# Attention operands of a backward pass packed in four groups of 32 rows, with the steps of the inner loop ordered by hand

## The chip, the cores and the metric

The kernel runs on one core of one Trainium2 chip. Times are device microseconds (us) of that core. A time that is quoted is the median of several executions, and "ratio" is always the mean time of one kernel's fast runs over the mean time of the other's fast runs of the same rounds, so it is not quite the ratio of the two medians.

The names of the engines in the profile are: PE is the matmul engine (PEld its weight loads), DVE is VectorE, ACT is ScalarE, POOL is GpSimd, and SP is SyncE.

## The reference

The reference is one transformer-like block and its gradients: `out = x + attention(xn) * silu(mlp(xn))` with `xn = layernorm(x)`, and the vector-Jacobian product of it for one `grad_out`. There are 2048 tokens, 512 features and 32 heads of 16 features. The part that matters here is the attention and its backward pass:

```python
def _A_ref(x, wqkv, wo):
    B, S, D = x.shape          # 1, 2048, 512
    H = 32
    Dh = D // H                # 16
    qkv = (x @ wqkv).reshape(B, S, 3, H, Dh).transpose(2, 0, 3, 1, 4)
    q, k, v = qkv[0], qkv[1], qkv[2]
    scores = jnp.einsum("bhqd,bhkd->bhqk", q, k) * (Dh ** -0.5)
    p = _softmax(scores, axis=-1)
    o = jnp.einsum("bhqk,bhkd->bhqd", p, v)
    return o.transpose(0, 2, 1, 3).reshape(B, S, D) @ wo
# ... layernorm, MLP, silu, and then
_out, _vjp = jax.vjp(_f, A_x, A_wqkv, A_wo, B_w1, B_b1, B_w2, B_b2)
_grads = _vjp(grad_out)
```

## The kernel before

The kernel has three phases: a first one up to about 285 us, the attention core up to about 2400 us, and a last one with the output projection and the weight gradients. The change touches only the attention core.

The core works through 64 blocks (16 pairs of heads times 4 chunks of 512 queries), and a block has 16 steps. Every step does the following, for both heads of the pair:

- `s`: the scores with keys on the rows, two matmuls into a tile of 128x1024 f32 (two PSUM banks). ScalarE makes `et = exp(s)`.
- `t`: the scores of the block before, with queries on the rows. ScalarE makes `e = exp(t)`.
- `d`: dP, the product of V and the output gradient, also 128x1024. VectorE makes `gts = d * et`.
- `X`: six accumulating matmuls, four on `et` and two on `gts`, into one bank for the whole block. At the block's end `X` is copied (`xs`), transposed on PE (`XT`), copied again (`xt`), and weights `W1`, `W2` for the next stage are made of it.
- `Z`: two matmuls on `e` and two on `gk`, which is `gts` transposed by a DMA. Every fourth step VectorE adds `Z` to `acc`.

So a step needs two exponentials of 128x1024, and one multiply of the same size. "The edge" below means positions 0 to 4 of a block, where `X` changes hands. PSUM is the memory that PE writes its results to; the kernel lays it out in 8 banks. A slot is one buffer in it: the next tile of that slot waits until the last one has been read (below, most `d` start 0.05 us after the multiply that reads the one before). A mode is how many rows and columns of PE's array a matmul takes, as the profile prints it: 64\*128 or 32\*128 for `s`, `t` and `d`, 128\*32 or 128\*17 for `X` and `Z`. A change of mode is one between these two kinds.

```python
# PSUM: 8 banks = s 2, (t and d share a ring of two slots) 4, X 1, Z 1
ps_s = ctx.enter_context(tc.tile_pool(name="ps_s", bufs=1, space=PSUM))
ps_x = ctx.enter_context(tc.tile_pool(name="ps_x", bufs=1, space=PSUM))
ps_z = ctx.enter_context(tc.tile_pool(name="ps_z", bufs=1, space=PSUM))
ps_d = ctx.enter_context(tc.tile_pool(name="ps_dt", bufs=2, space=PSUM))
ps_t = ps_d
# ... operands: per head 64 rows, K and V side by side; Q alone, dO alone
KVT=opnd.tile([128, S], bf16, name=f"KVT{i}"),
QT=opnd.tile([128, S], bf16, name=f"QT{i}"),
DOT=opnd.tile([128, S], bf16, name=f"DOT{i}"),

def emit_r1(g):                       # s, t, d of step g
    # ...
        s = ps_s.tile([128, 2, 512], f32, name="s")
        for hj in range(2):
            r0 = 64 * hj
            nc.tensor.matmul(s[:, hj, :], lhsT=op["KVT"][r0:r0 + 64, kb * 128:(kb + 1) * 128],
                             rhs=op["QT"][r0:r0 + 64, qc * 512:(qc + 1) * 512],
                             start=True, stop=True, tile_position=(r0, 0))
    # ...
        t = ps_t.tile([128, 2, 512], f32, name="t", tag="d")       # then two matmuls on QT, KVT
    # ...
        d = ps_d.tile([128, 2, 512], f32, name="d", tag="d")       # then two matmuls on KVT, DOT

def emit_mult(g):
    # ...
    nc.vector.tensor_tensor(out=gts[:, kb % 2], in0=st_d.pop(g)[:], in1=st_et[g], op=ALU.mult)

def emit_finalize(j):                 # at a block's end
    # ...
    XT = ps_x.tile([128, 4, 128], f32, name="XT", tag="X")         # in the one bank of X
    # ... four transposes, copy to xt, then W1 and W2

emit_r1(0)
for g in range(NSTEP + 16 + lagb + laga):
    # ...
    emit_r1(g + 1)                    # s, t, d of the next step
    emit_exp_a(g)                     # et
    emit_mult(g)                      # gts
    emit_exp_b(g)                     # e
    emit_dmat(g)                      # gk by DMA
    # ... X(et) of step g-1, Z, X(gts) of step g-1
```

Around this a scheduler decides the final order on each engine; in this kernel it leaves PE's order as s, t, d, X, Z.

## Time and profile before

| | before |
|---|---|
| time, median of 3 runs | 3007.36 us (3003.35 to 3009.01) |
| first and last start of an `e` exponential | 311.3 and 2391.9 us |
| one block, average | 32.54 us |
| ACT busy from 320 to 2350 us | 1875 of 2030 us |
| one exponential; pitch of two that queue | 1026 ns; 0.90 to 0.92 us |

The first fence shows lines of the page of the profiled execution of the kernel before: busy time and share of each engine, then the row of ACT in tenths in 40 slices, then the three costliest groups. In a group the columns are line, engine, operation, tiles and shapes, count, then busy us and mean ns of one, then idle time of the engine just before and what ended most of it.

```profile
...
PE 2491.3 (83%) x19909; PEld 859.6 (29%) x19968; DVE 2011.0 (67%) x2422; ACT 2205.8 (74%) x2485; POOL 583.2 (19%) x944
...
ACT  2442899998899999999999989999999824441020
...
L701 DVE TENSOR_TENSOR gts<-d,et 128x1024 bf16<-128x1024 f32 x1024 | 1251.5, 1222 | 555.9 <-ACT et L690 534.5
L690 ACT ACTIVATE et<-s 128x1024 bf16<-128x1024 f32 x1024 | 1050.5, 1026 | 161.5 <-PE s L647 126.7
L727 ACT ACTIVATE e<-t 128x1024 bf16<-128x1024 f32 x1024 | 1049.5, 1026 | 6.2 <-PE t L659 5.0
...
```

Over the whole span no engine stands out (PE 83%, ACT 74%). The row by slices says why this average is of no use: from the fifth slice to the 32nd, which is about the attention, ACT is at 80% or more. The windows view of the kernel before gives the same stretch in us; its columns are the window, its length, busy us and count for PE, PEld, DVE, ACT and POOL, then the granted PE clock, the share of the DMA engines and GB/s.

```profile
...
320.00:2350.00 2030.00, 1828.77 (x16108) 540.00 (x16109) 1495.49 (x1608) 1874.98 (x1983) 219.21 (x594) 1.00 0.81 146
...
```

ACT is busy 92% of that window, PE 90%. The exponentials overlap each other by some 0.1 us, so ACT is close to full; the leak is the rest. The waits view of the kernel before for the same window says what the leak is; the columns are total us, number of times, longest.

```profile
...
DVE gts L701 <- ACT et L690: 521.0, 696, 3.3
...
PE t L659 <- ACT e L727: 119.6, 450, 0.5
ACT et L690 <- PE s L647: 117.7, 172, 2.6
...
```

VectorE waits on ScalarE, which is as it should be with ScalarE the limit. The line that counts is the last: ScalarE, the limit, waited 118 us for `s`.

The timeline of the kernel before shows one pair of steps; columns are start us, duration us, engine, line, operation.

```profile
...
1118.60 1.22 DVE L701 TENSOR_TENSOR gts<-d,et 128x1024 bf16<-128x1024 f32 x1
...
1119.17 0.39 PE L647 MATMUL s<-QT_2217,KVT_2216 64*128 64x512 bf16 x2
...
1119.53 0.39 PE L659 MATMUL t<-KVT_2216,QT_2217 64*128 64x512 bf16 x2
...
1119.60 1.02 ACT L690 ACTIVATE et<-s 128x1024 bf16<-128x1024 f32 x1
1119.87 0.39 PE L670 MATMUL d<-DOT_2218,KVT_2216 64*128 64x512 bf16 x2
...
1120.52 1.02 ACT L727 ACTIVATE e<-t 128x1024 bf16<-128x1024 f32 x1
...
1120.66 1.22 DVE L701 TENSOR_TENSOR gts<-d,et 128x1024 bf16<-128x1024 f32 x1 [0.84 <-ACT et L690]
...
1120.96 0.39 PE L647 MATMUL s<-QT_2217,KVT_2216 64*128 64x512 bf16 x2
...
1121.43 1.03 ACT L690 ACTIVATE et<-s 128x1024 bf16<-128x1024 f32 x1
1121.59 0.39 PE L659 MATMUL t<-KVT_2216,QT_2217 64*128 64x512 bf16 x2 [0.24 <-ACT e L727]
...
1121.93 0.39 PE L670 MATMUL d<-DOT_2218,KVT_2216 64*128 64x512 bf16 x2
...
1123.02 0.39 PE L647 MATMUL s<-QT_2217,KVT_2216 64*128 64x512 bf16 x2
...
```

The first `s` at 1119.17 is followed by `t` 0.36 us and `d` 0.70 us later, and the next `s` is 1.79 us after it; but the third `s`, at 1123.02, comes 2.06 us after the second. And `t` at 1121.59 starts 0.05 us after the exponential of 1120.52 ends. Between 700 and 2000 us, 87% of all `d` start 0.053 us after the end of a multiply, and 87% of all `t` start 0.052 us after the end of an `e`.

### The profile page before, as it was taken

How to read it: one execution, taken by the hardware profiler on the slowest of the kernel's cores; microseconds unless marked ns; L12 is line 12 of the kernel's file. 1: busy time of each engine (PE TensorE's matmuls, PEld its weight loads, DVE VectorE, ACT ScalarE, POOL GpSimd, SP SyncE). 2: the span in 40 equal slices, each digit the busy share in tenths (PEclk: the TensorE clock that was granted, in tenths of full speed). 3: DMA queues.
4: the chain of work that ended last, by engine and by line, in shares of the span. 5: the costliest groups of instructions: out<-in, count | busy, mean ns of one | idle time of the engine just before them, and what ended most of it. 6: DMA issues, size and time to landing. Idle time of an engine off the chain costs nothing. (4 is left out here: it accounts for less than half of the span.)

```text
span 2997.4 us, 50127 instructions
## 1 busy us (share of the span) xinstructions
PE 2491.3 (83%) x19909; PEld 859.6 (29%) x19968; DVE 2011.0 (67%) x2422; ACT 2205.8 (74%) x2485; POOL 583.2 (19%) x944
## 2 busy tenths in 40 slices
PE   3786998898899899899988988998898865665967
PEld 2332222222222222222222222222222233332443
DVE  5764777777777777777777777777777637882044
ACT  2442899998899999999999989999999824441020
POOL 0334011101101110110111011011101026881024
PEclk8898999999999999999999999999999987887989
DMA  5436888869878886987888698788867563325431
GB/s 169 120 127 145 142 151 138 162 130 157 142 147 149 142 162 132 160 145 148 153 138 161 132 158 142 148 153 137 162 132 130 107 230 94 103 81 153 127 127 41
DMA packets 1324301, 417.62 MB, mean 139 GB/s; under 512 B 1247393, under 2 KB 1308194, under 8 KB 1324066
## 3 DMA queue, kind: packets, MB, share of 16 engines
q1 hardware_dynamic: 1250674, 360.80, 63.0%
q10 hardware_dynamic: 73392, 53.62, 5.8%
q8 instruction: 156, 2.56, 0.3%
q14 instruction: 79, 0.65, 0.1%
HBM read 65.41 MB, written 55.32 MB: 40 GB/s over the span
## 5 line engine op out<-in xcount | busy, mean ns | idle before, releaser
L701 DVE TENSOR_TENSOR gts<-d,et 128x1024 bf16<-128x1024 f32 x1024 | 1251.5, 1222 | 555.9 <-ACT et L690 534.5
L690 ACT ACTIVATE et<-s 128x1024 bf16<-128x1024 f32 x1024 | 1050.5, 1026 | 161.5 <-PE s L647 126.7
L727 ACT ACTIVATE e<-t 128x1024 bf16<-128x1024 f32 x1024 | 1049.5, 1026 | 6.2 <-PE t L659 5.0
L742 PE MATMUL X<-et,Lc 128*32 128x512 bf16 x2048 | 403.2, 389 | 2.3 <-DVE xt L776 0.2
L659 PE MATMUL t<-KVT_2216,QT_2217 64*128 64x512 bf16 x1024 | 200.5, 380 | 63.8 <-ACT e L727 61.4
L659 PE MATMUL t<-KVT_2222,QT_2223 64*128 64x512 bf16 x1024 | 200.1, 380 | 64.0 <-ACT e L727 61.3
L647 PE MATMUL s<-QT_2217,KVT_2216 64*128 64x512 bf16 x1024 | 201.3, 388 | 15.2 <-DMA QT_2217<-QPad 15.1
L670 PE MATMUL d<-DOT_2218,KVT_2216 64*128 64x512 bf16 x1024 | 201.0, 381 | 11.8 <-DVE gts L701 6.2
L670 PE MATMUL d<-DOT_2224,KVT_2222 64*128 64x512 bf16 x1024 | 200.4, 380 | 4.8 <-DVE gts L701 2.8
L647 PE MATMUL s<-QT_2223,KVT_2222 64*128 64x512 bf16 x1024 | 199.9, 387 | 0.0
L758 PE MATMUL X<-gts,NAT_2219 128*17 128x512 bf16 x1024 | 198.0, 381 | 0.0
L758 PE MATMUL X<-gts,NAT_2225 128*17 128x512 bf16 x1024 | 197.4, 381 | 0.0
L745 PE MATMUL X<-et,NAT_2219 128*32 128x512 bf16 x1024 | 196.8, 391 | 0.0
L745 PE MATMUL X<-et,NAT_2225 128*32 128x512 bf16 x1024 | 196.4, 390 | 0.0
L742 PEld LDWEIGHTS <-Lc 128*32 128x32 bf16 x2048 | 100.4, 93 | 245.1 <-issue 236.8
L659 PEld LDWEIGHTS <-QT_2223 64*128 64x128 bf16 x1024 | 89.2, 94 | 188.7 <-issue 188.5
L659 PEld LDWEIGHTS <-QT_2217 64*128 64x128 bf16 x1024 | 89.2, 94 | 185.8 <-issue 185.6
L837 DVE TENSOR_TENSOR acc<-Z,acc 64x512 f32<-64x512 f32 x192 | 129.3, 673 | 8.7 <-PE Z L829 8.7
L670 PEld LDWEIGHTS <-KVT_2216 64*128 64x128 bf16 x1024 | 90.0, 93 | 138.4 <-issue 127.9
L670 PEld LDWEIGHTS <-KVT_2222 64*128 64x128 bf16 x1024 | 90.6, 93 | 126.4 <-issue 118.6
L647 PEld LDWEIGHTS <-KVT_2216 64*128 64x128 bf16 x1024 | 52.1, 93 | 224.9 <-issue 223.7
L647 PEld LDWEIGHTS <-KVT_2222 64*128 64x128 bf16 x1024 | 49.1, 93 | 218.0 <-issue 218.0
(1527 smaller groups left out, 3829.7 us busy)
## 6 DMA issues: line engine op xcount, KB each, us to landing
gk<-gts SPq DMA_TRANSPOSE x512, 4.3
HG_s<-hg SPq DMA_DIRECT2D x16, 448.0 KB, 2.9
GB_s<-gB ACTq DMA_DIRECT2D x16, 256.0 KB, 2.0
dKVT_s<-ob SPq DMA_DIRECT2D x16, 256.0 KB, 3.6
dhc<-DH_s ACTq DMA_DIRECT2D x2, 2048.0 KB, 13.6
H1T_s<-h1row SPq DMA_DIRECT2D x14, 256.0 KB, 2.0
H1T_s<-h1row ACTq DMA_DIRECT2D x14, 256.0 KB, 2.0
h1T<-H1T_s SPq DMA_DIRECT2D x8, 448.0 KB, 3.8
```

The source lines that it names most:

```text
L647: nc.tensor.matmul(s[:, hj, :], lhsT=op["KVT"][r0:r0 + 64, kb * 128:(kb + 1) * 128], rhs=op["QT"][r0:r0 + 64, qc * 512:(qc + 1) * 512], st ...
L659: nc.tensor.matmul(t[:, hj, :], lhsT=op["QT"][r0:r0 + 64, q0:q0 + 128], rhs=op["KVT"][r0:r0 + 64, kc * 512:(kc + 1) * 512], start=True, st ...
L670: nc.tensor.matmul(d[:, hj, :], lhsT=op["KVT"][r0:r0 + 64, kb * 128:(kb + 1) * 128], rhs=op["DOT"][r0:r0 + 64, qc * 512:(qc + 1) * 512], s ...
L690: nc.scalar.activation(out=et, in_=st_s.pop(g)[:], func=ACT.Exp)
L701: nc.vector.tensor_tensor(out=gts[:, kb % 2], in0=st_d.pop(g)[:], in1=st_et[g], op=ALU.mult)
L727: nc.scalar.activation(out=e[:], in_=st_t.pop(g)[:], func=ACT.Exp)
L742: nc.tensor.matmul(X[64 + 32 * hj:64 + 32 * hj + 32, :], lhsT=Lc[:, :], rhs=et[:, hj, :], start=(kb == 0), stop=False, skip_group_check=Tr ...
L745: nc.tensor.matmul(X[32 * hj:32 * hj + 32, :], lhsT=NATt[:, kb, hj, 1:33], rhs=et[:, hj, :], start=(kb == 0), stop=(kb == 15), tile_positi ...
L758: nc.tensor.matmul(X[64 + 32 * hj:64 + 32 * hj + 17, :], lhsT=NATt[:, kb, hj, 0:17], rhs=gts[:, kb % 2, hj, :], start=False, stop=(kb == 1 ...
L837: nc.vector.tensor_tensor(out=av, in0=Z[0:64, :], in1=av, op=ALU.add)
```

## The change

The intent is to let `s` and `d` run side by side on PE and to take the waits out of PE's order. K of both heads and V of both heads are packed in four groups of 32 rows (K0, K1, V0, V1), Q and dO likewise, so that `s` uses rows 0 to 63 and `d` rows 64 to 127. The steps are put in an order by hand, with the scheduler off. `d` gets two slots of one bank each, where it shared two slots of two banks with `t` before; `s` and `t` now share such a pair. The multiply is split in two halves to match. `XT` moves into a `d` slot. Some casts move from VectorE to POOL.

```diff
-    ps_s = ctx.enter_context(tc.tile_pool(name="ps_s", bufs=1, space=PSUM))
+    ps_st = ctx.enter_context(tc.tile_pool(name="ps_st", bufs=2, space=PSUM))
+    ps_d = ctx.enter_context(tc.tile_pool(name="ps_d", bufs=2, space=PSUM))
-    ps_d = ctx.enter_context(tc.tile_pool(name="ps_dt", bufs=2, space=PSUM))
-    ps_t = ps_d
# ...
-            QT=opnd.tile([128, S], bf16, name=f"QT{i}"),
-            DOT=opnd.tile([128, S], bf16, name=f"DOT{i}"),
+            QDT=opnd.tile([128, S], bf16, name=f"QDT{i}"),
# ... d, by halves of one bank
+        for hj in range(2):
+            r = 64 + 32 * hj
+            d = ps_d.tile([128, 512], f32, name="d", tag="d")
+            nc.tensor.matmul(d[:], lhsT=op["KVT"][r:r + 32, kb * 128:(kb + 1) * 128],
+                             rhs=op["QDT"][r:r + 32, qc * 512:(qc + 1) * 512],
+                             start=True, stop=True, tile_position=(r, 0))
# ... et in an order by query blocks (a strided output)
+        nc.scalar.activation(out=et[:, :, kb % 4, :, :].rearrange("k b h q -> k h b q"),
+                             in_=st_s.pop(g)[:].rearrange("k h (b q) -> k h b q", b=4), func=ACT.Exp)
# ...
-        XT = ps_x.tile([128, 4, 128], f32, name="XT", tag="X")
+        XT = ps_d.tile([128, 4, 128], f32, name="XT", tag="d")
# ... the loop
-        emit_r1(g + 1)
-        # ...
-        emit_exp_a(g)
-        emit_mult(g)
-        emit_exp_b(g)
-        emit_dmat(g)
-        # ... X(et), Z, X(gts) of step g-1
+        first = g % 16 == 1
+        emit_t(g)
+        if not first:
+            emit_le(g - 1)            # X on et
+        emit_exp_b(g)
+        emit_s(g + 1)
+        emit_d(g)
+        emit_mult(g)
+        emit_exp_a(g + 1)
+        emit_dmat(g)
+        if first:
+            emit_le(g - 1)
+        emit_g(g - 1)                 # X on gts
+        emit_z(g - lagb, 0)
+        emit_z(g - lagb, 1)
+        if g >= 17 and (g - 17) % 16 == 0 and (g - 17) // 16 < NB:
+            emit_finalize((g - 17) // 16)
# ... and with tc.manual_schedule(): around the call of attention_core
```

## The prediction

> **What bounds it now.** Attention runs from about 285 to 2392 us. It is 64 blocks of 16 steps; a steady step has two exponentials, one multiply dP*E, and PE groups s, t, d, X, Z. The tile view gives e starts from 311.3 to 2391.9 us: 32.5 us a block. In the timeline, exponentials that queue behind each other start 0.92 us apart (one takes 1026 ns, overlapping the next), so ScalarE's floor is 1.84 us a step, 29.4 us a block. In the windows view ACT is busy 1875 of the 2030 us from 320 to 2350. ScalarE is the limit, leaking 3 us a block. The waits view puts 118 us on exponentials waiting for PE's s (172 waits, up to 2.6 us). The timeline shows two leaks: (1) steps alternate 1.83 and 2.04 us, because PE issues s just ahead of t, t waits for the previous e, and d, X and Z stand between it and the next s; (2) at a block's edge X's single bank is held until XT is transposed and copied; gaps of 0.2 to 1.2 us follow.
>
> **What the change does.**
> - PE: s and d use four different 32-row groups and can run together. Pairs of s, t, d are now 0.32 to 0.36 us apart, groups in one column mode 0.22, a mode change 0.31: about 1.78 us a step without waits. After: s+d about 0.35 instead of 0.68, but four mode changes a step instead of two, about 0.1 us each. [...] PE sum 1.5 to 1.75.
> - Order: t, X(e), s, d, X(g), Z spreads t and s half a step apart, each just after the exponential that frees its slot, with 0.3 to 0.4 us slack. That should remove leak (1), about 100 us.
> - XT moves into a d slot, so X is freed after the xs copy (0.68 us). But XT waits for a multiply and delays t: I add up about 1.1 us a block.
> - DVE: one 1222 ns multiply becomes two of about 680 ns, starting 0.61 apart: +0.1 us. In all about 1.6 us a step. The loop d, two multiplies, next d is close to 1.84: 0.4 + 1.29 + semaphores. This is the thinnest margin.
> - ACT: same 2048 exponentials, one with strided output; no change per instruction. POOL takes the ob casts (32.5 us on DVE).
>
> **Prediction.** A block takes about 31.0 us instead of 32.5 (29.4, 1.1 at its edge, 0.5 for waits on d): 64 x 1.55, about 100 us less. 2905 us, range 2845 to 2975. Faster by over 2%: 0.75; within 2%: 0.22; slower: 0.03.
>
> **What would show it.** Right: ACT busy over 93% in attention, e starts about 31 us a block, waits of et for s well under 118 us, exponentials still 1026 ns and 0.92 apart, s and d starting within some 20 ns, paired multiplies 680 ns. Wrong: steady steps above 1.9 us with d waiting for gts; s and d one after another; exponentials over 1.03 us; long waits of t after XT.
>
> **What would make it wrong.** The d loop over 1.84 us, as its banks are freed only by both multiplies; mode changes costlier than 0.1 us; four weight loads serialised; a slower strided exponential (0.1 us costs 100 us); transposes late with four gts buffers instead of five.

Its 0.1 us for a mode change is the difference of the intervals that it quotes, 0.31 and 0.22 us. That `s` and `d` can run together, and that the halves of a multiply start 0.61 us apart, was not shown when it was written; the kernel after shows `s` and `d` 9 ns apart, and the halves, of 685 ns each, 0.61 us.

## The result, and the profile after

| | before, same rounds | after |
|---|---|---|
| time, median | 3006.62 us (3003.35 to 3009.01, 4 runs) | 2853.40 us (2852.69 to 2856.73, 4 runs) |
| ratio | | 0.9494 (95%: 0.9481 to 0.9508) |
| first and last `e` | 311.3 and 2391.9 us | 316.9 and 2257.2 us |
| one block, average | 32.54 us | 30.35 us |

The change makes the kernel faster by 153 us. The lines of the page of the kernel after, as shown of before:

```profile
...
PE 2409.6 (84%) x19968; PEld 864.4 (30%) x19968; DVE 2038.9 (71%) x3382; ACT 2161.5 (76%) x2485; POOL 619.2 (22%) x1023
...
ACT  2342799999999999999999999999999734440020
...
L697 DVE TENSOR_TENSOR gts<-d,et 128x512 bf16<-128x512 f32 x2048 | 1317.6, 685 | 370.9 <-ACT et L676 211.1
L684 ACT ACTIVATE e<-t 128x1024 bf16<-128x1024 f32 x1024 | 1085.1, 1061 | 64.4 <-PE t L634 63.9
L676 ACT ACTIVATE et<-s 128x1024 bf16<-128x1024 f32 x1024 | 1093.4, 1068 | 12.1 <-PE d L662 11.7
...
L662 PE MATMUL d<-QDT,KVT 32*128 32x512 bf16 x2048 | 450.0, 383 | 1.9
...
```

The multiply is now two of 685 ns each, at 1317.6 us in all instead of 1251.5. The idle column of the `et` group fell from 161.5 us to 12.1. Here is the windows view of the kernel after:

```profile
...
320.00:2200.00 1880.00, 1722.31 (x16011) 545.90 (x16010) 1513.57 (x2525) 1820.06 (x1972) 259.00 (x678) 1.00 0.86 153
...
```

ACT is now busy 96.8% of the window, with POOL and PE both lower than that. The waits view of the kernel after:

```profile
...
PE s L648 <- ACT et L676: 139.7, 611, 0.5
DVE gts L697 <- PE d L662: 104.0, 187, 0.9
ACT e L684 <- PE t L634: 59.3, 126, 1.7
...
```

No line of `et` waiting for `s` is left in this view. What ScalarE still waits for is `t`, 59 us in all over 126 waits. PE waits for ScalarE (140 us), which is harmless. The timeline of the kernel after, a step and a half:

```profile
...
1103.23 1.11 ACT L684 ACTIVATE e<-t 128x1024 bf16<-128x1024 f32 x1
...
1103.48 0.39 PE L648 MATMUL s<-QDT,KVT 32*128 32x512 bf16 x2 [0.20 <-ACT et L676]
...
1103.49 0.39 PE L662 MATMUL d<-QDT,KVT 32*128 32x512 bf16 x2
...
1104.01 1.29 DVE L697 TENSOR_TENSOR gts<-d,et 128x512 bf16<-128x512 f32 x2
...
1104.13 1.13 ACT L676 ACTIVATE et<-s 128x1024 bf16<-128x1024 f32 x1
...
1104.64 0.39 PE L634 MATMUL t<-KVT,QDT 32*128 32x512 bf16 x2
...
1105.13 1.05 ACT L684 ACTIVATE e<-t 128x1024 bf16<-128x1024 f32 x1
...
1105.31 0.39 PE L648 MATMUL s<-QDT,KVT 32*128 32x512 bf16 x2
...
```

`s` at 1103.48 and `d` at 1103.49 start together. The exponentials at 1103.23, 1104.13 and 1105.13 are 0.90 and 1.00 us apart, and each starts before the record of the one ahead of it ends. The `t` for the exponential at 1105.13 was issued at 1104.64, 1.16 us after `s`, and the next `s` follows 0.67 us later: the two producers are spread over the step.

To compare kernels, the time between two `e` starts was averaged for each of the 16 positions in a block. When exponentials queue in the kernel after, most of them start 0.904 us apart (some 0.92), so 1.807 us is taken as the floor of a step and 28.9 as that of a block. What lies over that floor is split in "within" (positions 5 to 15, less 11 times 1.807) and "edge" (positions 0 to 4, less 5 times 1.807). "Tail" is the time from the last `e` to the end. All are in us. The last 15 `e` have no `et` beside them, so the average block is some 0.2 us shorter than 28.9 and the two terms together.

| kernel | mean step, positions 5 to 15 | within | edge | average block | tail |
|---|---|---|---|---|---|
| before | 1.940 | 1.46 | 2.40 | 32.54 | 605.5 |
| after | 1.833 | 0.29 | 1.33 | 30.35 | 595.0 |

The two profiled executions differ by 145 us (2997.4 and 2852.2 us span; the one of before was some 8 us quicker against its median than the one of after). Of these, 140 us lie between the first and the last `e`, which the two terms share nearly equally: 1.17 us a block within, 1.07 at the edge. The tail is 10.5 us shorter, and the first `e` comes 5.6 us later.

The edge that is left in the kernel after looks like this in its timeline:

```profile
...
1114.28 1.06 ACT L684 ACTIVATE e<-t 128x1024 bf16<-128x1024 f32 x1
1114.37 0.68 DVE L750 COPY xs<-X 128x512 f32<-128x512 f32 x1
...
1115.10 0.39 PE L729 MATMUL X<-et,Lc 128*32 128x512 bf16 x2 [0.23 <-DVE xs L750]
...
1115.87 0.66 PE L760 MATMUL XT<-ident_f,xs 128*128 128x128 f32 x4
...
1116.45 0.39 PE L634 MATMUL t<-KVT,QDT 32*128 32x512 bf16 x2
1116.56 0.69 DVE L762 COPY xt<-XT 128x512 f32<-128x512 f32 x1 [0.26 <-PE XT L760]
...
1116.94 1.02 ACT L684 ACTIVATE e<-t 128x1024 bf16<-128x1024 f32 x1 [0.68 <-PE t L634]
...
```

`X` of the new block waits for the copy of the old one (`xs`, 1114.37 to 1115.05). The rest of `X` and `Z` follow, then `XT` at 1115.87, and only behind it comes `t` at 1116.45, so that the exponential at 1116.94 was 0.68 us late. `XT` does not wait for its `d` slot here: in all 63 blocks that another follows it starts 0.31 us behind the last `Z`, with no idle time of PE, when a multiply has freed the slot 0.16 us before. The second half of the next `d`, however, starts 0.05 us after the copy `xt` ends: it waits for the slot that `XT` holds.

### The profile page after: what moved, and what is told of

Same layout as the page of the kernel before. It is cut to its first block, busy times and chain, and to the rows that moved or that the text cites. A ratio compares the mean times of both kernels' runs of the same rounds, so it can differ in the third digit from the quotient of the medians.

```text
span 2852.2 us, 51396 instructions
## 1 busy us (share of the span) xinstructions
PE 2409.6 (84%) x19968; PEld 864.4 (30%) x19968; DVE 2038.9 (71%) x3382; ACT 2161.5 (76%) x2485; POOL 619.2 (22%) x1023
## 5 line engine op out<-in xcount | busy, mean ns | idle before, releaser
L697 DVE TENSOR_TENSOR gts<-d,et 128x512 bf16<-128x512 f32 x2048 | 1317.6, 685 | 370.9 <-ACT et L676 211.1
L684 ACT ACTIVATE e<-t 128x1024 bf16<-128x1024 f32 x1024 | 1085.1, 1061 | 64.4 <-PE t L634 63.9
L676 ACT ACTIVATE et<-s 128x1024 bf16<-128x1024 f32 x1024 | 1093.4, 1068 | 12.1 <-PE d L662 11.7
L648 PE MATMUL s<-QDT,KVT 32*128 32x512 bf16 x2048 | 404.4, 384 | 160.8 <-ACT et L676 144.6
L662 PE MATMUL d<-QDT,KVT 32*128 32x512 bf16 x2048 | 450.0, 383 | 1.9
L732 PE MATMUL X<-et,NAT 128*32 128x512 bf16 x2048 | 407.3, 395 | 0.0
L807 PE MATMUL Z<-e,W 128*32 128x512 bf16 x2048 | 402.0, 388 | 2.2 <-DVE acc L820 1.4
L744 PE MATMUL X<-gts,NAT 128*17 128x512 bf16 x2048 | 401.3, 388 | 0.0
L634 PE MATMUL t<-KVT,QDT 32*128 32x512 bf16 x2048 | 400.5, 382 | 0.5 <-ACT e L684 0.5
L813 PE MATMUL Z<-gk,W 128*32 128x512 bf16 x2048 | 394.7, 379 | 0.0
L648 PEld LDWEIGHTS <-KVT 32*128 32x128 bf16 x2048 | 161.4, 91 | 397.7 <-issue 396.3
L807 PEld LDWEIGHTS <-W 128*32 128x32 bf16 x2048 | 121.4, 93 | 54.2 <-issue 52.9
L820 DVE TENSOR_TENSOR acc<-Z,acc 64x512 f32<-64x512 f32 x192 | 129.0, 672 | 12.1 <-PE Z L813 12.1
L813 PEld LDWEIGHTS <-W 128*32 128x32 bf16 x2048 | 103.9, 96 | 7.5
L662 PEld LDWEIGHTS <-KVT 32*128 32x128 bf16 x2048 | 97.4, 91 | 0.9 <-issue 0.9
```

The lines of the kernel that those rows point to most:

```text
L634: nc.tensor.matmul(t[:, hj, :], lhsT=op["QDT"][r:r + 32, q0:q0 + 128], rhs=op["KVT"][r:r + 32, kc * 512:(kc + 1) * 512], start=True, stop= ...
L648: nc.tensor.matmul(s[:, hj, :], lhsT=op["KVT"][r:r + 32, kb * 128:(kb + 1) * 128], rhs=op["QDT"][r:r + 32, qc * 512:(qc + 1) * 512], start ...
L662: nc.tensor.matmul(d[:], lhsT=op["KVT"][r:r + 32, kb * 128:(kb + 1) * 128], rhs=op["QDT"][r:r + 32, qc * 512:(qc + 1) * 512], start=True, ...
L676: nc.scalar.activation(out=et[:, :, kb % 4, :, :].rearrange("k b h q -> k h b q"), in_=st_s.pop(g)[:].rearrange("k h (b q) -> k h b q", b= ...
L684: nc.scalar.activation(out=e[:], in_=st_t.pop(g)[:], func=ACT.Exp)
L697: nc.vector.tensor_tensor(out=gts[:, kb % 2, hj, :].rearrange("k (b q) -> k b q", b=4), in0=ds[hj][:].rearrange("k (b q) -> k b q", b=4), ...
```

## The experiments

The theory at the start was that the order does most of it, with the packing adding the parallel `s` and `d`. The rivals were that the packing as such, the split of `d`, the place of `XT`, or the clock of PE made the difference. Each experiment undoes or does one part. The kernel before ran beside each group of them: 3004.47 us beside unpacked, old_order, old_unpacked and packed_only; 3008.55 beside one_slot, xt_in_x, edge_t and gk_first; 3005.73 beside the rest. These medians differ by 4 us, so a difference of less than about 5 us between kernels of different groups says little.

### 1. The new order without the packing (unpacked)

```diff
# from the kernel after
-            QDT=opnd.tile([128, S], bf16, name=f"QDT{i}"),
+            QT=opnd.tile([128, S], bf16, name=f"QT{i}"),
+            DOT=opnd.tile([128, S], bf16, name=f"DOT{i}"),
# ... three padded transposes a pair again; s, t and d by 64 rows:
-            r = 32 * hj            # d: 64 + 32 * hj
+            r = 64 * hj
```

> The changed kernel with 64-row operands again (s, t, d on the same two row groups, three operand transposes a pair); its order, its d slots and XT's place are kept. Theory A (packing and order are both needed in this order, because four mode changes a step eat what slack there is): from the intervals of the two traces a step's PE work adds up to 0.32+0.32+0.34+0.32+0.22+0.31 = 1.83 us, over ScalarE's 1.81, so a steady step takes 1.85 to 1.90 us and the run 2890 to 2935 us. Rival B (the order alone removes the waits inside a block): steady step 1.81 to 1.84, run 2850 to 2875. Rival C (the packing is all of it): steady step back at 1.93 or more, run over 2960.

Measured: 2892.21 us (2890.00 to 2896.05), ratio 0.9629 (0.9614 to 0.9643). The mean step is 1.873 us, within 0.73, edge 1.43. `d` starts 0.215 us behind `s` instead of 9 ns. So order, slots and the other small parts (hand schedule, moved casts, strided output) give 112 us together without the packing, and the packing gives some 39 us more. The trace parts these 39: the loop is 33 us shorter with the packing (0.52 us a block times 64), mostly within the blocks; the tail is 14.5 us shorter (609.5 against 595.0), probably by where buffers lie in memory, as in experiment 8 (in unpacked, too, the load of `B_all` starts behind the last `Z`, at 2288.3 us; it was not tested there); and the first `e` comes 5.7 us later.

### 2. The packing with the old order (old_order, old_unpacked)

```diff
# from the kernel after; old_unpacked adds the edit of experiment 1
-    emit_exp_a(0)
+    emit_d(0)
# ...
-        emit_t(g)
-        if not first:
-            emit_le(g - 1)
-        emit_exp_b(g)
-        emit_s(g + 1)
-        emit_d(g)
+        emit_exp_a(g)
         emit_mult(g)
-        emit_exp_a(g + 1)
+        emit_exp_b(g)
         emit_dmat(g)
# ... the block's end here, then
+        emit_s(g + 1)
+        emit_t(g + 1)
+        emit_d(g + 1)
+        emit_le(g - 1)
+        emit_z(g - lagb, 0)
+        emit_z(g - lagb, 1)
+        emit_g(g - 1)
```

> The changed kernel, packed, with PE and ScalarE in the order of before: s, t, d, X(e), Z, X(g). XT is issued ahead of s, as it must be to get a d slot. Theory A (packing alone removes the alternate 0.2 us waits, because t and d now run together and the way from the end of e by t, d, X, Z to the next s falls from 1.43 to about 1.1 us): steady step 1.81 to 1.86 us, run 2850 to 2900. Rival B (the order is what removes them): steady step 1.92 to 1.96, run over 2950.

> Both undone: 64-row operands and the order of before, with the d slots, the split multiply and XT's place of the changed kernel. All theories of the order and the packing: the steady step returns to 1.92 to 1.97 us. The block's edge stays cheaper than before's 2.4 us if XT's place is what made it cheap: run 2930 to 2985; if the edge was cheapened by order or packing, run 2990 to 3020.

Measured: old_order 3643.34 us, ratio 1.2130 (1.2093 to 1.2168); old_unpacked 3309.59 us, ratio 1.1019 (1.1001 to 1.1038). Both are far slower than anything expected, and both are of little use. In these kernels the order of VectorE is by hand too, and the addition to `acc` stands between two multiplies while `Z` stands behind `d` on PE. So every fourth step there is a chain from multiply to `d`, `X`, `Z`, `acc` and the next multiply, and that step takes 3.1 us in old_unpacked. In the kernel before, the scheduler had put that addition one multiply later. (The first forms of these two kernels deadlocked when they were built, because `XT` asked for a `d` slot behind the next `d`.)

old_order has a second trouble. The windows view of old_order:

```profile
...
1000.00:1520.00 520.00, 451.31 (x3194) 101.57 (x3194) 301.88 (x501) 378.31 (x393) 51.86 (x134) 0.72 0.62 110
...
```

The granted clock is 0.72 here. In its timeline the matmuls that start from 1199.5 to 1201.4 us take 0.60 to 0.64 us, and those from 1201.9 to 1206.2 us 0.38 or 0.39, as in the kernels before and after. In the same window old_unpacked, with the same order on 64 rows, has a clock of 0.99, and the kernel after, on 32 rows like old_order, 1.00. So the comparison is confounded twice. What lowered the clock is open. As expected, `t` and `d` can start together with the packing: in the timeline of old_order `t` starts at 1202.17 and the first half of `d` at 1202.18 us.

### 3. The kernel before with nothing but the packing (packed_only)

```diff
# from the kernel before, scheduler and order as they were
-            QT=opnd.tile([128, S], bf16, name=f"QT{i}"),
-            DOT=opnd.tile([128, S], bf16, name=f"DOT{i}"),
+            QDT=opnd.tile([128, S], bf16, name=f"QDT{i}"),
# ... two padded transposes a pair; s and t by 32 * hj, d by 64 + 32 * hj, 32 rows each
```

> The kernel before with packed operands alone; its order, slots, XT in X's bank and scheduler are kept. Theory A (packing alone removes the waits inside a block, the edge is a matter of XT's place): steady step 1.81 to 1.87 us, edge still 2.2 to 2.6 us a block, run 2925 to 2955. Rival B (order): steady step 1.93 or more, run 2990 to 3015.

Measured: 3026.95 us (3025.05 to 3035.00), ratio 1.0081 (1.0063 to 1.0099). By itself the packing gains nothing and costs 0.8%. The timeline of packed_only shows why:

```profile
...
1180.54 1.23 DVE L695 TENSOR_TENSOR gts<-d,et 128x1024 bf16<-128x1024 f32 x1
...
1181.12 0.39 PE L641 MATMUL s<-QDT,KVT 32*128 32x512 bf16 x2
...
1181.47 0.39 PE L653 MATMUL t<-KVT,QDT 32*128 32x512 bf16 x2
...
1181.82 0.39 PE L664 MATMUL d<-QDT,KVT 32*128 32x512 bf16 x2
...
```

The rows of `t` and `d` differ now, and yet `d` at 1181.82 starts 0.35 us behind `t`: it starts 0.05 us after the multiply of 1180.54 ends, and 97% of all `d` between 700 and 2000 us do so. Freedom in the array was of no use here, where the output's slot was not free. The granted clock is 0.97 from 1000 to 1520 us (0.939 over the run, and about 0.95 to 0.96 in the others, old_order aside), so a part of the 0.8% can be the clock.

### 4. The multiply taken off `d` (no_d_before, no_d_packed)

```diff
# from the kernel before, and from packed_only; the result is wrong on purpose
-        nc.vector.tensor_tensor(out=gts[:, kb % 2], in0=st_d.pop(g)[:], in1=st_et[g], op=ALU.mult)
+        nc.vector.tensor_tensor(out=gts[:, kb % 2], in0=st_et[g], in1=st_et[g], op=ALU.mult)
```

> The kernel before, with the multiply taking E twice instead of dP and E (wrong result on purpose): nothing reads d any more, so PE's d never waits for a multiply. In before two ways round are of nearly the same length, 3.85 us for two steps: (i) e, t, d, X, Z, next s; (ii) s, et, multiply, d, X, Z, next s. Theory A (both bind): (i) is left, steady step 1.88 to 1.94 us, within 2% of before apart from the edge. Rival B (only (ii), the wait of d for the multiply, binds): steady step 1.81 to 1.85.

> The same in the kernel before with packed operands alone, whose steady step was 1.96 us although t and d may run together there. Theory A (packing shortens way (i) and leaves way (ii), which held it): with d's wait gone too, steady step 1.81 to 1.86 us and the run 100 us or more under packed_only's 3027, at most 2930. Rival B (the packed kernel in the old order is held by its clock or by its mode changes): steady step 1.92 or more.

Measured: no_d_before 2822.08 us (2819.74 to 2823.87), ratio 0.9392 (0.9378 to 0.9406), with a step of 1.819 us and an edge of 1.06; no_d_packed 2826.42 us (2825.22 to 2833.11), ratio 0.9411 (0.9396 to 0.9427), with 1.818 us and 1.07. These steps come closer to the floor of 1.807 us than those of any other kernel, and they do so in the old order. So PE's work, its changes of mode and its clock did not hold the old loop; the way over the slots and the multiply did.

It does not tell which slot. These two lines of the timeline of no_d_before show a `t` issued while ScalarE still reads the `t` before it:

```profile
...
1182.00 1.18 ACT L727 ACTIVATE e<-t 128x1024 bf16<-128x1024 f32 x1
...
1182.71 0.38 PE L659 MATMUL t<-KVT,QT 64*128 64x512 bf16 x2
...
```

In the kernel before this can't be, as `t` alternates with `d` in two slots. Here a `d` that nothing reads gives its slot back at once, and the next `t` takes it. So the experiment frees both waits, of `d` for the multiply and of `t` for the exponential. Its multiply is also shorter, 693 ns instead of 1222. Of the two ways round the old loop, the one over `t` and the one over the multiply, it clears both.

### 5. One two-bank slot for `d`, one multiply (one_slot)

```diff
# from the kernel after
-    ps_d = ctx.enter_context(tc.tile_pool(name="ps_d", bufs=2, space=PSUM))
+    ps_d = ctx.enter_context(tc.tile_pool(name="ps_d", bufs=1, space=PSUM))
# ... d is one tile [128, 2, 512] again, and the multiply one instruction of 128x1024;
# XT uses the first bank of such a slot
```

> The changed kernel with dP in one slot of two banks again and one multiply of 1024 columns; XT takes that slot. Theory A (the split is not what makes the steps faster: the way d, multiply, next d is then about 0.45 + 1.22 + 0.05 = 1.72 us, still under the 1.81 us of ScalarE): steady step 1.81 to 1.87 us; only the edge grows, as XT must wait for the whole multiply and d for the whole copy, by 0.5 to 1.0 us a block; run 2880 to 2925 us. Rival B (two one-bank slots are needed for the steady rate): steady step over 1.90, run over 2950.

Measured: 2880.53 us (2879.27 to 2884.70), ratio 0.9579 (0.9563 to 0.9595). The step is 1.831 us, unchanged from 1.833, but the edge is 1.75 us instead of 1.33. The split of `d` is worth 27 us, all of it at the edge, where `XT` no longer has to wait for a whole multiply: in the waits view of one_slot PE sits idle for that in 61 blocks, 25.5 us in all or 0.42 us a block, and in the kernel after not at all. In the waits view, ScalarE's waits for `t` go from 59 to 79 us.

### 6. `XT` back in the bank of `X`, the first `X` two steps late (xt_in_x, x_late)

```diff
# xt_in_x, from the kernel after
-        XT = ps_d.tile([128, 4, 128], f32, name="XT", tag="d")
+        XT = ps_x.tile([128, 4, 128], f32, name="XT", tag="X")
# ...
-        first = g % 16 == 1
+        first = g % 16 in (1, 2) and g < NSTEP + 16
# ... X of step 0 is issued after d of step 2, with X of step 1 behind it
-        if first:
+        if first and g % 16 == 2:
+            emit_le(g - 2)
+            emit_g(g - 2)
             emit_le(g - 1)
-        emit_g(g - 1)
+        if not (first and g % 16 == 1):
+            emit_g(g - 1)
# x_late: the same order, but XT in a d slot as in the kernel after
```

> The changed kernel with XT back in X's bank, so that the next block's X starts one step later, behind the copy of XT. Theory A (XT's place made the edge cheaper): the edge, now about 1.3 us a block over the floor, returns to 2.0 to 2.6 us, run 2895 to 2940 us, steady step unchanged at 1.83. Rival B (the edge is cheaper by the order, whose slack takes a late X in): edge 1.0 to 1.5 us, run within 15 us of 2853.

> The run with XT in X's bank, instruction for instruction in the same order, but with XT in a d slot as in the changed kernel. It tells apart why XT in X's bank was 29 us faster. Theory A (the order: the next block's first X group behind XT, so that XT and the next t come earlier): 2820 to 2832 us, as with X's bank. Theory B (the slot: XT waits for a multiply, and d for the copy of XT): 2842 to 2860 us.

Measured: xt_in_x 2824.56 us (2821.66 to 2825.68), ratio 0.9389 (0.9374 to 0.9404); x_late 2840.83 us (2839.42 to 2844.18), ratio 0.9456 (0.9440 to 0.9472). The theory that the move of `XT` into a `d` slot made the edge cheap fell here: with `XT` back in the bank of `X` the kernel is 29 us faster than after, and its edge is 0.93 us instead of 1.33. x_late parts the two edits. By the medians some 12 of the 29 us come with the order (`X` goes behind `XT`, so PE does not wait for the copy in front of `XT`), and some 16 with the slot. The traces correct the first figure: from the first to the last `e` x_late is only 5 us shorter than the kernel after, and 6 us are its earlier first `e` (310.7 us against 316.9), which the edit does not touch. Between x_late and xt_in_x the same stretch shrinks by 20 us. In x_late `XT` comes early enough to wait for a multiply, and then `d` waits for the copy of `XT` (20.8 and 17.1 us in its waits view); in xt_in_x both waits are gone.

### 7. `XT` behind `t` (edge_t)

```diff
# from the kernel after
         emit_t(g)
+        if g >= 18 and (g - 18) % 16 == 0 and (g - 18) // 16 < NB:
+            emit_finalize((g - 18) // 16)
# ... and the same call at the end of step 17 taken out
```

> The changed kernel with XT's transposes issued after the next step's t instead of ahead of it. If the wait of t behind XT is what the edge costs (the timeline shows one gap of 0.7 us and one of 0.2 to 0.3 us a block), that gap goes, but s and d come later behind XT and d waits for the copy of XT: I expect about 0.45 us a block less, 2815 to 2840 us. If the edge is set by d and the copy of XT and not by t, no change, within 10 us.

Measured: 2875.54 us (2867.14 to 2878.41), ratio 0.9555 (0.9537 to 0.9574), so 22 us slower than after instead of faster. ScalarE's waits for `t` fell only from 59 to 49 us, and the longest from 1.7 to 0.8 us, but now `d` has to wait until the copy of `XT` has freed its slot, so the edge grew to 1.60 us. The wait was moved, not removed.

### 8. The place of `gk` in memory (gk_first)

```diff
# from the kernel after
+    gbp = sb("gbp", 6)
     etp = sb("etp", 3)
     gtp = sb("gtp", 4)
-    gbp = sb("gbp", 6)
```

> The changed kernel with the pool of gk created ahead of those of et and gts, which moves addresses alone: the loads of g_all and B_all for the next phase then overlap gk buffers that the last Z matmuls read, as they do in the kernel before. Theory A (10 us of the gain are memory placement, since these loads start 14 us before the end of attention instead of 3 us after the last e): the loads start within 3 us of the last Z, the first matmul with wo waits about 10 us for its weights, and the run is 8 to 14 us longer, 2861 to 2867. Rival B (the end of the attention is quicker for another reason): no change, within 4 us.

Here the question was the 10 us that the tail gained. In the kernel before, the loads of `g_all` and `B_all` for the last phase are issued at 2395.3 us, directly behind the last `Z` (2395.22), because their memory overlaps that of a `gk` buffer. In the kernel after, the buffers fall otherwise, and the loads are issued at 2245.2 us, 14 us ahead of the last `Z` (2259.31). The first matmul that needs `wo_sb`, which is loaded behind them, waited 10.33 us before and 0.31 us after.

Measured: 2859.58 us (2855.34 to 2865.91, 5 runs), ratio 0.9511 (0.9491 to 0.9530). The loads are at 2251.8 us again, 0.03 us behind the last `Z`; the same matmul waits 10.93 us, and comes 16.9 us after the last `Z` instead of 4.0. From the last `Z` to the end it takes 606.0 us instead of 592.9. So the place in memory is worth 13 us in the tail. The net is only some 5 us, too little to be told from noise (the two 95% intervals overlap), because the attention of this kernel ended 7.6 us earlier: its first `e` came 3.2 us sooner and its blocks were 0.07 us shorter. The first `e` varies from 310.7 to 316.9 us between kernels whose start has not been touched, so that part tells nothing; the rest is not explained.

### 9. One `t` of sixteen by DMA (x_unit)

```diff
# from xt_in_x: an option of the new code, switched on for one unit of 16;
# its e is made by a DMA transpose of et
-    dma_units = ()
+    dma_units = ((1, 3),)
```

> XT in X's bank, and one of the 16 second exponentials of a block replaced by a DMA transpose of E (the kernel's own option for one unit, with the t matmul gone too). If ScalarE bounds the steady rate, a block is shorter by up to 0.9 us: 2765 to 2800 us. If something else does (PE, the loop of d and the multiplies, or the DMA queues, at 0.88 of their time), 2815 us or more.

Measured: 2818.62 us (2817.17 to 2824.54), ratio 0.9384 (0.9370 to 0.9399), only 6 us better than xt_in_x, and their ratios (0.9384 and 0.9389) overlap. It was to save one exponential a block, 0.9 us. From 320 to 2200 us ACT is busy 1803 us instead of 1851, so the exponentials are gone, but the time is lost to a new wait. The timeline of x_unit at such a step:

```profile
...
1018.09 0.37 PE L662 MATMUL d<-QDT,KVT 32*128 32x512 bf16 x1
1018.55 0.67 DVE L820 TENSOR_TENSOR acc<-Z,acc 64x512 f32<-64x512 f32 x1
1018.68 0.37 PE L662 MATMUL d<-QDT,KVT 32*128 32x512 bf16 x1 [0.23 <-DVE gts L697]
...
1019.81 0.39 PE L634 MATMUL t<-KVT,QDT 32*128 32x512 bf16 x2
...
1020.30 1.02 ACT L684 ACTIVATE e<-t 128x1024 bf16<-128x1024 f32 x1 [0.78 <-PE t L634]
...
```

Without the `t` in this step the order has no slack. The second half of `d` waits for a multiply (1018.09 to 1018.68), the addition to `acc` stands between two multiplies, `t` comes at 1019.81, and the exponential at 1020.30 finds ScalarE idle for 0.78 us. The saved 0.9 us is given back nearly whole. The share of the DMA engines from 320 to 2200 us also rose, to 0.93 from 0.88 in xt_in_x; whether it binds was not tested. x_unit and xt_in_x are the fastest kernels that give the right result.

## Why the prediction was right or wrong

**Right: direction, range and limit.** 2905 us was forecast, 2853 measured, inside 2845 to 2975. ScalarE is the limit and is now busy 96.8% of the attention.

**Right: leak (1) goes away.** The waits of `et` for `s`, 118 us before, are not listed any more. But the reason given was too short. The prediction named the wait of `t` for the exponential alone. The wait of `d` for the multiply ties with it (87% each), and packed_only shows that wait holding `d` when the array would allow `d` beside `t`. The new order cures both at once: `d` stands beside the next step's `s`, a step behind its own `et`. Which wait alone would have held the kernel before is open, as experiment 4 frees both.

**Right: packing runs `s` and `d` side by side.** They start 9 ns apart, against 0.215 us in unpacked. In the traces of before and after, groups of `X` and `Z` behind one another are mostly 0.22 us apart and groups with a change of mode between them mostly 0.31 to 0.33, so the prediction's 0.1 us for a change held. The packing is worth 39 us of 2892 under the new order (33 of them in the loop), and costs 0.8% under the old one, since PE was not what held the loop (experiment 4).

**Right: the multiply.** 685 ns each, two in a row start 0.61 us apart, and pairs take 1.29 us. The loop over `d`, called the thinnest margin, does not bind: the mean step is 1.833 us against a floor of 1.807. The margin is thin all the same: between 700 and 2000 us 89% of the second halves of `d` start 0.05 us after a multiply ends, some 0.03 us behind the first halves.

**Right as to cost, wrong as to reason: the edge.** 1.1 us a block was forecast and 1.33 measured. The prediction saw a gain in moving `XT` into a `d` slot; x_late against xt_in_x shows that the slot costs some 16 us once the order lets `XT` come early. It also had `XT` wait for a multiply, which it doesn't do in the kernel after. Given that slot, the split of `d` makes the edge 0.42 us a block cheaper (one_slot) and the packing 0.10 (unpacked). That the order and its slack do the rest is left over by elimination, and not shown by a run.

**A sign that misled.** The prediction took exponentials over 1.03 us as a sign of trouble. They are 1061 and 1068 ns on average in the kernel after, up to 1.13 us while they queue, and yet start 0.904 us apart. In the kernel before queued ones overlap by 0.10 to 0.13 us, in the kernel after by up to 0.21 us. So the longer record was no loss here; it is the pitch that has to be read. The strided output cost nothing that shows.

**The size: 100 us forecast, 153 measured.** The terms that were mis-sized, each a block times 64:

| term | forecast | measured | effect |
|---|---|---|---|
| ScalarE's floor | 29.4 us (pitch 0.92) | 28.9 us (pitch 0.904) | 31 us |
| waits within the block | 0.5 us | 0.29 us | 13 us |
| edge | 1.1 us | 1.33 us | -15 us |
| last block without `et`, left out of the sum | 0 | -0.19 us | 12 us |
| tail | unchanged | 10.5 us shorter | 10 us |
| first `e` | unchanged | 5.6 us later | -6 us |
| profiled execution against median | | | 8 us |

They add up to 53 us, which is the miss. The largest is the floor: 16 ns a pitch count 2048 times. The 0.92 us were read rightly off the kernel before. Of its exponentials whose scores had been ready for over 0.365 us, 724 of 728 start about 0.92 us after the one ahead. In the kernel after, where scores come later, 1368 of 2047 start 0.904 us after the one ahead, and most of those ready for over 0.365 us again 0.92. That the pitch would shorten could not be seen before, and why it does is open: in no_d_before 427 with scores ready that long start 0.904 us apart. The tail was not in the prediction at all. It is a change of addresses that let loads start early, and gk_first shows it.

**Open.** What the order and the scheduling by hand are each worth as such (no kernel for either was run without a confounder), what sets the pitch of the exponentials at 0.904 or 0.92 us, why the blocks of gk_first were a little shorter, and what lowered the clock in old_order and packed_only.

## What to carry to other kernels

Where one engine is the limit, look for the waits that it ends up in, and put each producer half a step ahead of it, just behind the event that frees its slot; in this kernel that gave 112 of the 153 us, together with the new slots, the hand schedule and the moved casts. Let matmuls run side by side only after the slots of their outputs are free at the same time: the same packing was worth 33 us in the loop under the new order and cost 0.8% under the old one. After a gain, test each part alone, since a part that looked like the cause can be a cost (`XT` in a `d` slot, 16 us).
